# A gated attention with a feed-forward block on one core: the orders of three engines as written lists

## The chip, the core and the metric

The kernel runs on one core of a Trainium2 chip. The core has five engines with instruction streams of their own: TensorE (PE in the profile) multiplies matrices and transposes, VectorE (DVE) and ScalarE (ACT) work element by element, GpSimd (POOL) does the same and issues some loads, SyncE (SP) issues most transfers. Each engine runs its instructions strictly in the order in which the program holds them; engines wait for each other by semaphores. The metric is the device time of one execution in microseconds (us).

## The reference

Two blocks follow each other, in float32. The first is a gated linear recurrence for 4 batches of 8 heads, 768 time steps and 48 features: a complex decay per step and feature, and a state of 48 x 48 per head. The second is a feed-forward block on the 3,072 tokens that come out (384 wide, 1,024 hidden).

```python
mag = np.sqrt(a_re * a_re + a_im * a_im)
scale = np.minimum(mag, 0.999) / (mag + 1e-06)
a_re_n, a_im_n = (a_re * scale, a_im * scale)
for t in range(S):
    ar, ai = (a_re_n[:, :, t, :, None], a_im_n[:, :, t, :, None])
    new_re = ar * S_re - ai * S_im
    new_im = ar * S_im + ai * S_re
    kv = np.einsum('bhd,bhe->bhde', k[:, :, t], v[:, :, t])
    S_re, S_im = (new_re + kv, new_im)
    y[:, :, t] = np.einsum('bhd,bhde->bhe', q[:, :, t], S_re)
...
h = (x @ w1) * (x @ w2) @ w3
out = h @ w_out
```

## The kernel before

The tokens are cut into eight **units**, u = 0 to 7: unit u is half a batch, 384 tokens, in three chunks of 128. Each unit has these parts.

- **Gate chain** (VectorE and ScalarE by turns; `gates_apart` and `gates`): from the loads re and im of the decay it makes the running magnitude and angle, and from them and from q and k four products: gR and k (key with cosine and sine), gA and q (query with cosine and sine). A unit's chain runs while TensorE works on the unit before.
- **Moves** (SyncE): twelve transfers per unit bring the products into the layouts KL (from gR and k) and QL (from gA and q) that the scores read; pieces of V are moved too (`turn_vr`).
- **Attention on TensorE**, per chunk: transposes tp of gR and of k, copied by ScalarE to KT (L993); kv, the product of KT and V, added to a state T; scores sc of KL and QL, copied through a mask to A by VectorE (L1007); and y from A, V, QL and T, copied by ScalarE to xT (units 0 to 2) or x.
- **Feed-forward on TensorE**: products m with w1 and w2 (L1089), copied and multiplied to ab by ScalarE (L1101, L1123, L1130) and VectorE (L1105), then o with the fused weight w3o (L1184) and a store. From unit 3 on, w1 and w2 are used as a coarse part wh and a remainder low; ScalarE and VectorE split them once, beside unit 2 (L1152, L1155, L1157).

Ahead of all that stands the **weight product** w3 times w_out (`fuse`, L1451): eight steps f of eight products, each with a piece wo_s of w_out and a slice w3s of w3. Both are loaded as raw words by SyncE and rounded first: VectorE takes signs and shifted words (L1236, L1248, L1250), ScalarE the low ends (L1241, L1244), VectorE adds them (L1253, "ISA" in the order). w3s has two buffers, so the slice of step f + 2 is written where that of step f was read.

What sets the order: TensorE's program order is written out by the code. For ScalarE, VectorE and SyncE the order in the weight product was left to a scheduler of the language, with order-only dependences that keep ScalarE's steps of one function table together (`chain`); in the units an account of times in the program (`run`, `book`, the table `TIMES`) decides between which copies a step of the gate chain, a rounding, a split or a move is put, and the code is emitted in that order inside a `manual_schedule`.

## Time and profile before

| | us |
|---|---|
| median of 3 runs | 533.48 |
| lowest and highest | 533.29, 538.1 |
| span of the profiled execution | 534.5 |
| TensorE busy | 498.3 (93%) |
| VectorE busy | 374.7 (70%) |
| ScalarE busy | 325.6 (61%) |
| GpSimd busy | 254.0 (48%) |

The profile is of one execution, with the line numbers of the kernel before. A row names the engine, the line, what is written <- what is read, the tile's shape and, in brackets, the idle time ahead of the instruction with what ended it. Busy time of TensorE is made of matmuls that overlap, so it isn't TensorE at its peak. The profile also states TensorE's granted clock as a share of full speed; a mean under 1.00 holds stretches at half.

### The profile page before, as it was taken

What the parts mean: (1) busy time and instruction counts of PE and PEld (TensorE: products, weight loads), DVE (VectorE), ACT (ScalarE), POOL (GpSimd) and SP (SyncE); (2) the same over time, 40 slices, a digit from 0 to 9 for tenths busy, and PEclk for the clock granted to TensorE, in tenths of its full rate; (3) what the DMA queues carried; (4) which work ended last, traced back from release to release, by engine and by line L of the source; (5) the groups of instructions that cost most, each with busy time, mean ns of one, the idle gap of its engine ahead of it and who ended that gap; (6) DMA issues with size and microseconds to landing.
All of it is one profiled execution on the core that took longest, in us unless ns stands there. A gap on an engine that the chain in (4) does not pass through costs nothing.

```text
span 534.5 us, 13643 instructions
## 1 busy us (share of the span) xinstructions
PE 498.3 (93%) x5594; PEld 378.1 (71%) x5594; DVE 374.7 (70%) x607; ACT 325.6 (61%) x569; POOL 254.0 (48%) x317
## 2 busy tenths in 40 slices
PE   5689889999998999988999999999999998999995
PEld 2355565556655679957888688967896787878972
DVE  7999699855779988756773876577657837336750
ACT  6979866665675458982587557855786554213420
POOL 1000000028968886752664765487457458415510
PEclk9899999999999999998999999999999999999999
DMA  8999859692379219791599239932993176716611
GB/s 258 369 400 286 189 161 307 126 232 72 79 174 229 73 56 234 157 219 40 126 236 216 77 82 245 225 90 70 229 232 87 40 209 169 205 43 189 200 50 37
DMA packets 66424, 89.75 MB, mean 168 GB/s; under 512 B 29872, under 2 KB 53872, under 8 KB 65584
## 3 DMA queue, kind: packets, MB, share of 16 engines
q1 hardware_dynamic: 57904, 59.15, 44.0%
q0 software_dynamic: 8448, 29.63, 20.3%
q8 instruction: 46, 0.75, 0.6%
q14 instruction: 26, 0.21, 0.1%
HBM read 61.01 MB, written 4.72 MB: 123 GB/s over the span
## 4 chain that ended last, share of the span: by engine, by line
PE 51%; DVE 17%; DMA 13%; issue 6%; ACT 5%; POOL 5%; SPq 1%; POOLq 0%; DVEq 0%; ACTq 0%
PE m L1089 24%; PE o L1184 16%; PE y L1043 4%; PE sc L1004 4%; DMA k<-in_k_dram 3%; DMA KL<-k 3%; PE kv L1069 2%; DVE gR L750 2%; PE tp L991 2%; DMA QL<-q 2%; DMA q<-in_q_dram 2%; DMA look<-in_a_re_dram 1%; DVE gA L753 1%; DMA raw<-in_w_dram 1%; POOL look L1327 1%
## 5 line engine op out<-in xcount | busy, mean ns | idle before, releaser
L1184 PE MATMUL o<-w3o,ab 128*128 128x384 f32 x384 | 131.7, 492 | 0.0
L1089 PE MATMUL m<-x,low 128*128 128x384 f32 x576 | 119.2, 339 | 0.0
L1089 PEld LDWEIGHTS m<-x,low 128*128 128x128 f32 x576 | 102.6, 188 | 0.2 <-ACT m L1123 0.2
L1184 PEld LDWEIGHTS o<-w3o,ab 128*128 128x128 f32 x384 | 70.4, 190 | 45.6 <-issue 2.4
L1105 DVE TENSOR_TENSOR ab<-m,ab 128x384 f32<-128x384 f32 x64 | 35.1, 553 | 57.2 <-PE m L1089 39.4
L1089 PE MATMUL m<-x,wh 128*128 128x384 f32 x288 | 69.6, 350 | 3.4 <-ACT ab L1130 2.4
L1123 ACT ACTIVATE m<-m 128x384 f32<-128x384 f32 x96 | 45.5, 476 | 36.0 <-PE m L1089 35.6
L1089 PE MATMUL m<-xT,ws 128*128 128x384 f32 x192 | 63.1, 487 | 1.2 <-ACT xT L1054 1.2
L1328 POOL TENSOR_SCALAR look<-look 128x192 f32<-128x192 f32 (+1 forms) x55 | 54.4, 988 | 5.0
L1089 PEld LDWEIGHTS m<-x,wh 128*128 128x128 f32 x288 | 50.8, 188 | 7.4 <-ACT ab L1130 3.6
L1325 POOL TENSOR_TENSOR look<-look 128x256 f32<-128x256 f32 (+1 forms) x43 | 31.9, 743 | 50.1 <-DMA look<-in_w_dram 32.3
L1089 PEld LDWEIGHTS m<-xT,ws 128*128 128x128 f32 x192 | 36.0, 190 | 25.6 <-ACT xT L1054 1.7
L1273 POOL MEMSET seen<- 128x256 bf16 x1 | 0.3, 317 | 107.7 <-DVE ab L1105 107.7
L1007 DVE COPY_PREDICATED A<-mask,sc 128x512 f32<-128x512 uint8 x48 | 32.8, 734 | 26.5 <-PE sc L1004 26.5
L1289 POOL TENSOR_TENSOR seen<-seen,look 128x192 bf16<-128x192 bf16 (+1 forms) x55 | 44.3, 805 | 4.5
L1051 POOL TENSOR_TENSOR x<-x,x 128x384 fp32r<-128x384 f32 x18 | 23.1, 1284 | 41.7 <-DVE x L1050 41.5
L1188 ACT COPY ot<-o 128x384 f32<-128x384 f32 x24 | 11.4, 476 | 48.4 <-PE o L1184 48.2
L1043 PE MATMUL y<-A,V 128*32 128x128 f32 x768 | 40.2, 276 | 0.6 <-issue 0.6
L1004 PEld LDWEIGHTS sc<-QL,KL 96*32 96x32 f32 x1536 | 29.2, 112 | 13.6 <-issue 8.7
L1004 PE MATMUL sc<-QL,KL 96*32 96x32 f32 (+3 forms) x1536 | 32.8, 238 | 4.4 <-DMA QL<-q 3.0
L1043 PEld LDWEIGHTS y<-A,V 128*32 128x32 f32 x768 | 35.0, 112 | 1.5 <-issue 1.5
L1043 PE MATMUL y<-QL,T 96*32 96x128 f32 x640 | 35.6, 275 | 0.0
(163 smaller groups left out, 909.2 us busy)
## 6 DMA issues: line engine op xcount, KB each, us to landing
looked<-in_w_dram POOLq DMA_DIRECT2D x14, 512.0 KB, 4.5
look<-in_w_dram POOLq DMA_DIRECT2D x27, 256.0 KB, 5.0
raw<-in_w_dram SPq DMA_DIRECT2D x6, 1024.0 KB, 10.3
KL<-gR SPq DMA_DIRECT2D x24, 192.5 KB, 3.6
KL<-k SPq DMA_DIRECT2D x24, 192.5 KB, 7.1
QL<-gA SPq DMA_DIRECT2D x24, 192.0 KB, 8.2
QL<-q SPq DMA_DIRECT2D x24, 192.0 KB, 7.9
raw<-in_w_dram SPq DMA_DIRECT2D x6, 768.0 KB, 6.1
```

Source lines behind the costliest of these rows:

```text
L1004: nc.tensor.matmul(out=sc[SB * g:SB * g + SB, j, s0:C], lhsT=KL[:, x * n + j, w][:, s0:s0 + SB], rhs=QL[:, x * n + j, w][:, s0:C], start=T ...
L1007: last["sc", u, c, x] = nc.vector.copy_predicated(out=A[:, x * n:(x + 1) * n], data=sc, mask=mask)
L1043: nc.tensor.matmul(out=o, lhsT=a, rhs=b, start=s0, stop=s1)
L1051: nc.gpsimd.tensor_tensor(out=x[2], in0=x[1], in1=x[0], op=OP.subtract)
L1089: nc.tensor.matmul(out=out, lhsT=a, rhs=b, start=start and i == 0, stop=i == len(terms) - 1, skip_group_check=not start)
L1105: last["ab", u, j] = nc.vector.tensor_tensor(out=ab_t[u][:, j], in0=m, in1=ab_t[u][:, j], op=OP.mult)
L1123: nc.scalar.activation(out=got[m], in_=got[m], func=AF.Copy, scale=1.0 + 1.0 / BITS)
L1184: nc.tensor.matmul(out=m, lhsT=ab_t[u][:, f, t * P:(t + 1) * P], rhs=w3o[:, f], start=(f == 0), stop=(f == KF - 1))
L1188: nc.scalar.copy(out=o, in_=m)
L1289: nc.gpsimd.tensor_tensor(out=seen[:, 0:n], in0=seen[:, 0:n], in1=x, op=OP.add)
L1325: tt(out=x, in0=x, in1=x, op=OP.mult)
L1328: ts(out=x, in0=x, scalar1=low, scalar2=None, op0=OP.is_ge)
```

## The change

Every call on `nc.scalar`, `nc.vector`, `nc.gpsimd` and `nc.sync` is now recorded, in the order of the code. At the end `in_order` reads a list of numbers for each engine: n over 0 takes the call n places behind the first that is left, n under 0 takes the next -n as they stand. Between each call and the next on the same engine it sets an order-only dependence, over the whole kernel, the weight product included. The list of GpSimd is empty, so its calls stay as recorded. The dependences of `chain` and the inner `manual_schedule` are gone. All recorded calls now carry the line of the recorder (L385).

```diff
--- before.py
+++ after.py
@@ -375,6 +375,69 @@
         f()
 
 
+class Log:
+
+    def __init__(self, engine):
+        self.engine, self.log = engine, []
+
+    def __getattr__(self, name):
+        def call(*args, **kw):
+            self.log.append(getattr(self.engine, name)(*args, **kw))
+            return self.log[-1]
+        return call
+
+
+class Logged:
+
+    def __init__(self, nc):
+        self.nc = nc
+        self.scalar, self.vector, self.gpsimd, self.sync = (Log(e) for e in (nc.scalar, nc.vector, nc.gpsimd, nc.sync))
+
+    def __getattr__(self, name):
+        return getattr(self.nc, name)
+
+
+ORDERS = dict(
+    scalar="""
+9 -10 5 -5 2 2 2 -1 1 1 8 2 -1 1 -1 1 -8 3 -1 3 -1 4 1 1 1 -2 3 -1 3 -2 4 -1 3 3 -3 6 6 6 -3 3 3 3 -1 2 1 1 -2 4 -3
...
+""", vector="""
+-2 11 4 4 4 9 1 1 -1 6 -1 4 -8 1 -2 11 -1 1 -1 7 -1 6 -1 2 -1 1 8 8 -4 5 4 -3 5 -1 5 4 1 1 2 2 3 -3 1 1 17 2 5 1 1 3
...
+""", gpsimd="""
+
+""", sync="""
+-3 8 -4 1 -2 3 -3 1 -1 7 -1 6 3 3 3 -1 2 2 1 1 1 -1 2 20 -4 18 18 20 17 21 21 17 2 15 5 16 2 7 4 2 12 5 3 4 2 2 2 4
...
+""")
+
+
+def in_order(tc, log, order):
+
+    left, before, taken = list(log), None, []
+    for n in map(int, order.split()):
+        taken += [left.pop(n)] if n > 0 else [left.pop(0) for _ in range(-n)]
+    for ins in taken + left:
+        if before:
+            tc.add_manual_dep(ins.ins, before.ins.name, ORDER, reason="order")
+        before = ins
+
+
 @with_exitstack
 def tile_gateloop__then__multiplicative_ffn_kernel(
     ctx: ExitStack,
@@ -413,7 +476,7 @@
 
 
 
-    nc = tc.nc
+    plain, nc = tc.nc, Logged(tc.nc)
     B, H, D, S = qt.shape
     P = 128
     C = 128
@@ -452,7 +515,7 @@
     weights_pool = ctx.enter_context(tc.tile_pool(name="weights", bufs=1))
     w3o = weights_pool.tile([P, KF, DM], FP, name="w3o")
     ident = weights_pool.tile([P, P], FP, name="ident")
-    make_identity(nc, ident)
+    make_identity(plain, ident)
     good = weights_pool.tile([1, 1], I32, name="good")
 
     fast = ExitStack()
@@ -598,8 +661,6 @@
 
     def chain(ins):
 
-        if chained and not paced:
-            tc.add_manual_dep(ins.ins, chained[-1].ins.name, ORDER, reason="tables")
         chained[:] = [ins]
 
     def gate_head(u):
@@ -1767,7 +1828,7 @@
         fills = [("f7", lambda j=j: [fuse(KF - 1, j + x) for x in range(2)]) for j in range(KF // 2, KF, 2)]
         gate["ops"] = gates(1, False)
         chain(nc.scalar.preload_act_table_set("natural_log_exp_and_others"))
-        with tc.manual_schedule(engines={mybir.EngineType.Activation, mybir.EngineType.DVE, mybir.EngineType.Pool, mybir.EngineType.SP}):
+        if True:
 
             paced.append(True)
             clock.update(PE=0.0, ACT=0.0, DVE=0.0, POOL=0.0, SP=3.0, DMA=8.0)
@@ -1797,9 +1858,11 @@
             seq += ffn(NU - 1)
             advance()
             run(seq[:-4] + [("judge", 0)] + seq[-4:-2] + [("judge", 1)] + seq[-2:])
+    for name, order in ORDERS.items():
+        in_order(tc, getattr(nc, name).log, order)
     fast.close()
 
-    value = nc.values_load(good[0:1, 0:1], min_val=0, max_val=1)
+    value = plain.values_load(good[0:1, 0:1], min_val=0, max_val=1)
     with tc.If(value == 0):
         general(tc, qt, kt, v, art, ait, w1, w2, w3t, wo, w3o, ident, out)
 
```

The number of instructions on each engine stays as it was, and so do the orders of TensorE and GpSimd. On VectorE 513 of 586 instructions stand in another place, on ScalarE 432 of 559, on SyncE 194 of 247, most of them by fewer than ten.

ScalarE in unit 0, at the end of the weight product (KT are the copies of the transposes; gA, re and gZ here are steps of unit 1's gate chain, low is a weight's low end). Before:

```order
L1455 ACTIVATE w3o<-f 128x384 x2
L993 COPY KT<-tp 128x128x3
L783 ACTIVATE gA<-re 128x3x384
L993 COPY KT<-tp 128x128x3
L783 ACTIVATE re<-gA 128x1152
L993 COPY KT<-tp 128x128x3
L1241 ACTIVATE low<-raw 128x512
L1073 COPY T_122<-kv 96x8x48
L993 COPY KT<-tp 128x128x3 x2
L783 ACTIVATE gZ<-gZ,consts 128x1152
L993 COPY KT<-tp 128x128x3
```

and after:

```order
L385 ACTIVATE w3o<-f 128x384
L385 COPY KT<-tp 128x128x3
L385 ACTIVATE low<-raw 128x512
L385 COPY KT<-tp 128x128x3 x2
L385 COPY T_122<-kv 96x8x48
L385 COPY KT<-tp 128x128x3 x3
L385 ACTIVATE w3o<-f 128x384
L385 ACTIVATE low<-raw 128x256
L385 ACTIVATE w3o<-f 128x384
L385 ACTIVATE low<-raw 128x256
L385 ACTIVATE w3o<-f 128x384 x2
```

The six KT copies stand ahead of the gate steps, which come later, behind the next copies w3o.

VectorE at step f = 2 of the weight product (w3s<-raw are the signs of the next slice, w3s<-w3s,low and wo_s<-wo_s,low the last step of the rounding). Before:

```order
L835 TENSOR_SCALAR gA<-gA 128x384
L838 SCALAR_TENSOR_TENSOR gA<-gA,gZ 128x384
L1253 ISA w3s<-w3s,low 128x2048
L1253 ISA wo_s<-wo_s,low 128x768
L1248 TENSOR_SCALAR w3s<-raw 128x1024
L853 TENSOR_TENSOR gZ<-gA,gR 128x384
L1236 TENSOR_SCALAR low<-raw 128x384
```

and after:

```order
L385 SCALAR_TENSOR_TENSOR gA<-gA,gZ 128x384
L385 TENSOR_SCALAR gA<-gA 128x384
L385 TENSOR_SCALAR w3s<-raw 128x1024
L385 ISA w3s<-w3s,low 128x2048
L385 ISA wo_s<-wo_s,low 128x768
L385 SCALAR_TENSOR_TENSOR gA<-gA,gZ 128x384
L385 TENSOR_SCALAR low<-raw 128x384
```

The signs of the slice for f = 3 moved from behind the two roundings for f = 2 to ahead of them.

SyncE in unit 3 (KL and QL are the moves that the scores need, V the moves of v's pieces, im and re loads for the next units). Before:

```order
L740 DMA KL<-gR 16x8x385 x3
L527 DMA im<-in_a_im_dram 128x3x384
L740 DMA KL<-k 16x8x385 x3
L740 DMA QL<-gA 16x8x384 x3
L740 DMA QL<-q 16x8x384 x3
L1190 DMA out_dram<-ot 128x384 x3
L527 DMA re<-in_a_re_dram 128x3x384
```

and after:

```order
L385 DMA KL<-gR 16x8x385
L385 DMA QL<-gA 16x8x384
L385 DMA V<-vr 64x6x48
L385 DMA KL<-gR 16x8x385 x2
L385 DMA KL<-k 16x8x385 x2
L385 DMA QL<-gA 16x8x384 x2
L385 DMA QL<-q 16x8x384 x3
L385 DMA KL<-k 16x8x385
L385 DMA V<-vr 64x6x48
L385 DMA V<-vr 32x6x48 x2
L385 DMA im<-in_a_im_dram 128x3x384
```

im moved from ahead of nine of the moves to behind all twelve, and three of V's pieces, which all stood ahead of the moves, stand behind them, one among them.

## Rows read from the trace of the kernel before

**Rows 1.** The page's first part: span, busy time of each engine.

```profile
span 534.5 us, 13643 instructions
...
PE 498.3 (93%) x5594; PEld 378.1 (71%) x5594; DVE 374.7 (70%) x607; ACT 325.6 (61%) x569; POOL 254.0 (48%) x317
```

**Rows 2.** The list of TensorE's waits: total us, times, longest us.

```profile
PE sc L1451 <- DVE wo_s L1253: 12.6, 5, 6.6
PE kv L1069 <- ACT KT L993: 3.8, 3, 2.2
PE sc L1004 <- DMA QL<-q: 3.0, 1, 3.0
PE m L1089 <- ACT ab L1130: 2.4, 3, 1.0
PE tp L991 <- DVE gR L750: 1.6, 3, 0.7
...
PE tp L991 <- ACT KT L993: 1.0, 3, 0.6
PE tp L991 <- DVE k L758: 1.0, 2, 0.7
PE m L1089 <- DVE ab L1105: 0.8, 2, 0.4
```

**Rows 3.** Windows: us, busy of PE, PEld, DVE, ACT, POOL, TensorE's clock, DMA.

```profile
240.00:280.00 40.00, 37.16 (x512) 32.57 (x513) 28.99 (x39) 23.30 (x46) 20.90 (x24) 0.96 0.56 132
```

**Rows 4.** Timeline of TensorE, 0 to 40: start, us, operation [idle before, what ended it].

```profile
17.49 2.31 PE L1451 MATMUL sc<-wo_s,w3s 128*128 128x384 f32 x4 [3.12 <-DVE wo_s L1253]
...
25.89 1.56 PE L1451 MATMUL sc<-wo_s,w3s 128*128 128x384 f32 x4 [1.27 <-DVE wo_s L1253]
...
37.85 1.56 PE L1451 MATMUL sc<-wo_s,w3s 128*128 128x384 f32 x4 [1.38 <-DVE wo_s L1253]
```

**Rows 5.** Timeline of VectorE, 24 to 26.

```profile
24.16 1.20 DVE L1253 CUSTOM_DVE_ANT_0 w3s<-w3s,low 128x2048 uint16<-128x2048 uint16 x1
25.28 0.55 DVE L1253 CUSTOM_DVE_ANT_0 wo_s<-wo_s,low 128x768 uint16<-128x768 uint16 x1
25.75 0.69 DVE L1248 TENSOR_SCALAR w3s<-raw 128x1024 int32<-128x1024 int32 x1
```

**Rows 6.** DMA of the first 26.5 us: the line of totals.

```profile
DMA packets 3460, 8.31 MB, mean 314 GB/s; under 512 B 379, under 2 KB 1899, under 8 KB 3179
```

**Rows 7.** Timeline of ScalarE, 57 to 60.

```profile
57.65 1.16 ACT L783 ACTIVATE gA<-re 128x1152 f32<-128x1152 f32 x1
58.71 0.55 ACT L993 COPY KT<-tp 128x384 f32<-128x384 f32 x1
```

**Rows 8.** Timeline of ScalarE, 165 to 167.

```profile
165.32 0.84 ACT L1152 ACTIVATE wh<-ws 128x768 fp32r<-128x768 f32 x1 [1.28 <-DVE low L1155]
166.07 0.54 ACT L993 COPY KT<-tp 128x384 f32<-128x384 f32 x1
```

**Rows 9.** Timeline of SyncE's DMA queue, 222 to 236: start, time of issuing.

```profile
223.54 0.60 SPq L527 DMA_DIRECT2D im<-in_a_im_dram  x1
...
229.82 3.88 SPq L740 DMA_DIRECT2D QL<-q  x3
```

**Rows 10.** DMA of 222 to 236 us: GpSimd's queue, packets, MB, share.

```profile
q0 software_dynamic: 173, 0.58, 15.8%
```

**Rows 11.** Timeline of VectorE, 60 to 106.

```profile
60.33 1.36 DVE L807 TENSOR_TENSOR im<-im,re 128x1152 f32<-128x1152 f32 x1 [4.03 <-ACT re L783]
...
72.93 1.37 DVE L1007 COPY_PREDICATED A<-mask,sc 128x512 f32<-128x512 uint8 x2
...
104.16 1.36 DVE L962 TENSOR_TENSOR gR<-k,re 128x1152 f32<-128x1152 f32 x1 [2.11 <-ACT re L783]
```

**Rows 12.** Timeline of TensorE, 111 to 112.

```profile
111.43 0.49 PE L991 MATMUL tp<-ident,gR 128*128 128x128 f32 x3
```

18 rows, old and new, of the table scalar are left out of this document.

## Prediction

> **What bounds the kernel now.** I read the page's busy shares first: TensorE (PE) is busy 498.3 of 534.5 us [rows 1]. The reader should see that the end is set by TensorE, and that an order of the other engines can win only two things: the time in which TensorE stands still, and the time in which it runs at the lower of its two clock levels after it stood still. Next comes the list of TensorE's waits [rows 2]; with its few smaller rows it sums to 29.7 us. The first 6.6 us of that are the wait for the first weights, so 23.1 us are to be had. Some 6.0 of these are the rest of the wait for rounded w_out weights (12.6 less 6.6) in the weight product ahead of the first unit; 17.1 us are spread over the eight units. Third I read the engine that ends each large wait, in order of time, to see what it did just before.
>
> The profiled execution's span is 534.5 us, 0.2% over the median of the runs, 533.48 us. I make the sum against 534.5 and take 1.0 us off at the end.
>
> **The change part by part.** TensorE's order and GpSimd's order stay as they were, and no instruction is added: order-only dependences between instructions of one engine need no semaphore. So no term is paid for the lists themselves, and every matmul keeps its duration. What moves is who stands in front of whom on ScalarE, VectorE and SyncE.
>
> *KT copies.* TensorE waits 3.8 us at kv and 1.0 us at tp for ScalarE's copies of transposed keys [rows 2], 4.8 us together. In unit 0 a copy of 0.55 us starts at 58.71, behind a gate step of 1.16 us that began at 57.65 [rows 7]; the other copies of this unit stand behind a second such step. The list puts all six copies of the unit ahead of both steps. In unit 2 the copy at 166.07 stands behind a weight split (wh) that itself waited 1.28 us for VectorE [rows 8]; this is the longest of the KT waits, 2.2 us. The list puts the copies of this chunk ahead of those splits. What is late next in unit 0 is a low end of a weight that now stands between the first and the second copy and waits for VectorE. I take 4.1 us of 4.8; bounds 2.5 and 4.8, since VectorE's steps may now come late where the copies were.
>
> *Moves in unit 3.* The longest wait among the units is 3.0 us at the scores for QL<-q [rows 2]. SyncE issues the 576 KB load of the next unit's im at 223.54, in front of nine of the twelve moves of KL and QL; the last three, QL<-q, start to issue at 229.82 [rows 9]. The list puts im behind all of them, and three of the V pieces behind them too, one among them. im fed only a chain that starts after the scores. I take 2.7 us of 3.0; bounds 0 and 3.0. With the wait goes the drop of the clock behind it: the mean granted clock of 240 to 280 us is 0.96 where it is 1.00 in stretches without such a wait [rows 3]; 4% of 40 us is 1.6 us at most, and I take 1.3.
>
> [...]
>
> *Small waits of the later units.* gR 1.6, m for ab of ScalarE 2.4, k 1.0, m for ab of VectorE 0.8 [rows 2]: 5.8 us in ten waits of 0.3 to 1.0 us, each a copy or a gate product that comes just late behind a neighbour. The list moves most of these by two to seven places, the copies forward and the gate steps back or the other way. Some go and some new ones come: 2.5 us, bounds 0 and 5.8. What is left of the 17.1 us (less 4.8, 3.0 and 5.8 it is 3.5, waits for score copies, xT and the like) I count with 0.6.
>
> Sum of gains: 4.1 + 2.7 + 1.3 + 2.5 + 0.6 = 11.2 us.
>
> *The head, a loss.* The eight steps f of the weight product each need a rounded w_out piece. The second, f=1, starts at 17.49 after a wait of 3.12 us, f=2 at 25.89 after 1.27, f=4 at 37.85 after 1.38 [rows 4]. The list on SyncE puts the 1,024 KB load of w3 for f=2 in front of the w_out load for f=1. In this stretch the queues moved 314 GB/s on average [rows 6], and that holds the empty first microseconds; 1.05 MB is 3.3 us at that rate, and I take 2.6 as the rate once it runs is higher. So f=1 starts 2.6 us later. VectorE then rounds f=2: before, w3s (1.20 us, from 24.16), wo_s (0.55, from 25.28), and after both the signs of f=3 (0.69, from 25.75) [rows 5]. The list puts these signs in front. They write the buffer that the last product of f=1 reads, so they cannot start before that product ends, and TensorE must then wait for 0.69 + 1.20 + 0.55, about 2.4 us, where it waited 1.3 [rows 4]: 1.2 us more. Against that, w3 of f=4 is loaded seven places earlier, and the wait ahead of f=4, 1.4 us, goes. Net loss 2.6 + 1.2 - 1.4 = 2.4 us. Bounds: a gain of 2.5, if the loads of f=1 overlap so that w_out lands as before and the early loads close the later waits; a loss of 4.
>
> The clock was lower behind the first of these waits: the four matmuls at 17.49 took 2.31 us, the four at 25.89 took 1.56 [rows 4]. That loss is there already, and I add none for the longer wait.
>
> *Unit 1, a loss.* VectorE began unit 1's gate chain at 60.33, behind an idle stretch of 4.03 us that ScalarE's gate steps ended [rows 11]. In the list the chain's first steps stand 19 to 24 places later, behind all score copies of unit 0, the last pair of which ran from 72.93 to 74.3 [rows 11]. The result gR began at 104.16 and took 1.36, so it was there at 105.5 [rows 11]; TensorE asks for it at 111.43 [rows 12], 5.9 us of slack. The start moves by 13 to 14 us. But VectorE stood still between its steps in this stretch, 2.11 us directly ahead of gR [rows 11], and weight roundings that used to stand between the chain's steps now stand ahead of them; the work from the chain's start to gR is about 34 us, so it ends at 108 if nothing stands still, and later by each wait for ScalarE. In the list gR also stands behind two ab products that are bound to TensorE's last matmuls ahead of the transposes, so it is just in time at best. I take a loss of 1.5 us; bounds 0 and 7.7 (13.6 less 5.9). Another 0.5 us is for units 2 and 3, where weight splits and chain are interleaved anew.
>
> Sum: 534.5 - 11.2 + 2.4 + 1.5 + 0.5 = 527.7 us of span, and 526.7 us as a median.
>
> **Rivals.** A run of this kernel tells about 1% from no change, so faster means under 528.1 and slower over 538.8.
>
> (a) The forecast, chance 0.56, own range 521 to 532; some two thirds of it lie under 528.1.
>
> (b) Nearly all waits of the units close: all 17.1 us and the 1.6 of the clock, with the head as it was: 534.5 - 18.7 = 515.8, with the head's loss 518.2; as a median 515 to 517. For it speaks that each large wait is removed by a move that leaves the waiting engine free; against it that the ten small ones have ten different neighbours. Chance 0.14.
>
> (c) The waits only change places: QL<-q lands no sooner, since the 16 DMA engines are busy in that stretch anyway, and the small waits come back elsewhere. Then 4.0 and 2.5 drop from the gains: 534.5 - 4.7 + 4.4 = 534.2, as a median 533. For it: a fixed list makes an engine stand behind a step that is late, and there are ten such interlocks in every unit. Against: KT and QL waits are each ended by one plain neighbour. Chance 0.18. It covers also that the lists do no more than write down nearly the same order: most instructions move by under ten places.
>
> (d) Slower: unit 1's gate chain. If none of the 13.6 us is won back, TensorE waits 7.7 us at unit 1's transposes. VectorE then runs behind, unit 2 repeats about half, 4, and two waits of this length drop the clock twice, 1.6 each. 534.5 - 11.2 + 2.4 + 7.7 + 4 + 3.2 = 540.6, as a median 539.6. It decides as soon as gR of unit 1 comes more than about 6 us after TensorE asks. For it: 34 us of work in 34 us of room. Against: VectorE's idle time in that stretch. Chance 0.12.
>
> **The numbers.** The predicted time is that of (a), 526.7. The range that leaves out (d), and the lower edge of (b), is 515.5 to 536. Faster: 0.38 of (a) and 0.14 of (b), 0.52. Same: 0.18 of (a) and 0.18 of (c), 0.36. Slower: 0.12.
>
> **What would show it.** KT copies: no wait at kv over 0.5 us in units 0 and 2. Moves: no wait for QL<-q and a clock of 1.00 in that unit. Head: f=1 starts near 20 us, a wait of about 2.4 us ahead of f=2, none ahead of f=4. Unit 1: gR ends close to the point at which the transposes ask, with a new wait of one or two us. The prediction falls if f=1 starts no later than before, or if the transposes of unit 1 wait for gR by more than 4 us.

## The result and the profile after

The changed kernel is slower: 541.98 us (median of 4 runs, 540.37 to 542.26) beside 533.38 us (4 runs, 533.17 to 538.1) for the kernel before on the same chip. The ratio is 1.0136, interval [1.0088, 1.0183]. The forecast was 526.7 us, so the time lies outside the range, on the side of the least likely rival. The medians of the kernel before differ from chip to chip (533 to 541 us), so below each ratio is to the runs of before beside it; the changed kernel was timed only beside the 533, so the experiments are compared with it in us and by their traces.

The page of the changed kernel, beside [rows 1]:

```profile
span 538.5 us, 13607 instructions
...
PE 502.6 (93%) x5594; PEld 382.1 (71%) x5594; DVE 374.5 (70%) x607; ACT 324.0 (60%) x569; POOL 254.9 (47%) x317
...
q8 instruction: 46, 0.75, 0.6%
```

The work is the same, and TensorE is still the bound. That its busy time grew by 4.3 us with the same 5,594 matmuls means a slower clock (a mean of 0.973 beside 0.993). The list of TensorE's waits, beside [rows 2] (engine, line, what ended the wait: total us, times, longest):

```profile
PE sc L1512 <- DVE wo_s L385: 16.8, 3, 7.2
PE sc L1065 <- issue: 5.4, 2, 3.5
PE y L1104 <- issue: 2.2, 1, 2.2
PE m L1150 <- ACT xT L385: 1.3, 2, 0.7
PE sc L1512 <- DVE w3s L385: 1.3, 1, 1.3
PE kv L1130 <- ACT KT L385: 1.2, 2, 0.7
PE sc L1065 <- DVE A L385: 0.8, 3, 0.3
PE tp L1052 <- ACT w3o L385: 0.4, 1, 0.4
PE m L1150 <- DVE ab L385: 0.3, 1, 0.3
```

Nearly every wait that the lists aim at is gone: QL<-q, gR, k and ScalarE's ab have no row any more. Two places have grown: the weight product ahead of the first unit (wo_s, 12.6 to 16.8 us), and a kind of wait that no engine and no load of data ends, "issue": 7.6 us where before had 0.6 in its whole list.

How far TensorE is behind can be read at the products kv, which both kernels run in the same order. It is 6.4 us late at the first kv of unit 0 (59.31 before, 65.72 after), 16.3 at that of unit 1 (115.53, 131.80), 18.0 at that of unit 2 (169.01, 187.05), then 11.1 at that of unit 4, 4.2 at the last of unit 7 (461.04, 465.26), and 4.2 at the end of the last matmul (528.50, 532.72). So **the lists lose 18 us in the first 190 us and win 13.8 back afterwards**. The timeline of TensorE, at the places of the loss, and where kv and the scores of unit 3 stand (start, us, operation, in brackets the idle time ahead of it):

```profile
22.06 2.93 PE L1512 MATMUL sc<-wo_s,w3s 128*128 128x384 f32 x4 [7.14 <-DVE wo_s L385]
...
31.39 2.38 PE L1512 MATMUL sc<-wo_s,w3s 128*128 128x384 f32 x4 [2.39 <-DVE wo_s L385]
...
44.92 1.56 PE L1512 MATMUL sc<-wo_s,w3s 128*128 128x384 f32 x4 [1.25 <-DVE w3s L385]
...
80.76 1.50 PE L1065 MATMUL sc<-QL,KL 96*32 96x64 f32 x39 [3.54 <-issue]
...
89.08 0.27 PE L1104 MATMUL y<-A,V 128*32 128x128 f32 x1 [2.23 <-issue]
...
127.67 0.52 PE L1052 MATMUL tp<-ident,gR 128*128 128x128 f32 x3
...
131.80 0.88 PE L1130 MATMUL kv<-vr,KT 128*32 128x48 f32 x48 [0.70 <-ACT KT L385]
...
146.40 0.77 PE L1065 MATMUL sc<-QL,KL 96*32 96x64 f32 x33 [1.90 <-issue]
...
256.20 1.32 PE L1065 MATMUL sc<-QL,KL 96*32 96x128 f32 x64
```

The first three rows answer to [rows 4], tp to [rows 12]; the last is where QL<-q was waited for. Windows of the same kernel, 240 to 280 being that of [rows 3] (us, busy us of PE, PEld, DVE, ACT, POOL, TensorE's granted clock, share and GB/s of the DMA engines):

```profile
59.00:89.00 30.00, 22.98 (x496) 17.25 (x495) 18.18 (x35) 14.02 (x25) 0.00 (x0) 0.89 1.07 258
...
79.80:86.60 6.80, 5.84 (x127) 5.81 (x128) 4.45 (x6) 0.65 (x2) 0.00 (x0) 0.50 1.09 241
90.10:96.80 6.70, 6.12 (x21) 3.24 (x13) 1.36 (x1) 3.00 (x4) 0.00 (x0) 0.50 0.75 188
148.10:151.40 3.30, 3.30 (x6) 1.35 (x4) 2.96 (x6) 0.00 (x0) 3.10 (x4) 0.50 0.10 30
240.00:280.00 40.00, 39.51 (x604) 30.92 (x603) 27.05 (x39) 22.97 (x43) 25.11 (x30) 1.00 0.59 133
```

And one of the kernel before:

```profile
59.00:89.00 30.00, 26.83 (x548) 19.20 (x549) 27.21 (x44) 22.87 (x33) 0.00 (x0) 1.00 0.73 216
```

From 59 to 89 us the DMA engines are full after the change (1.07, packets overlapping on an engine count twice) and had room before (0.73). Within that stretch TensorE stands still twice for "issue", and behind each such wait its clock is at half (0.50) for 6.8 us. The kernel before has this twice, for 3.4 us each: at 18.2 behind the wait ahead of f=1, and at 243.4 behind that for QL<-q; elsewhere, but for its last microsecond, its clock is 1.00. From kv of unit 0's last chunk to kv of unit 1's first the lag grows by 10.9 us, from 5.4 to 16.3. The two waits less the 0.6 of before are 5.1 us; the two stretches at half clock, 5.84 and 6.12 us busy, cost about half of that, 6.0, by estimate from the 0.50. Together 11.1.

What TensorE waits for there is, by the times, a block of its own instructions. The DMA view shows a queue of kind "instruction" (q8) that moves 46 packets of 16 KB in the whole run; TensorE's 11,188 matmuls and weight loads make 243 to a packet. One such packet moves at 78.09 to 79.35, and TensorE goes on at 80.76; one at 86.53 to 87.71, and it goes on at 89.08; one at 144.09 to 145.06, and it goes on at 146.40. The first of these in the DMA view of 78.0 to 79.4 (queue: packets, MB, share):

```profile
q1 hardware_dynamic: 209, 0.41, 98.1%
q8 instruction: 1, 0.02, 5.6%
```

The data queue next to it is full.

The other traces bear this out, and show when a block is asked for. TensorE's order is the same in every run, so its matmuls and weight loads can be counted. In all 17 profiles the waits for issue of over 0.5 us, 20 of them, stand at four places of that order (about the 695th, the 951st, the 1,199th to 1,205th and the 1,957th to 1,963rd instruction), some 250 apart or a multiple of it, and each ends 2.2 to 2.7 us after such a packet starts to move. The packet that is needed at one place seems to be asked for one block earlier: where the queues have room it moves at about the time that TensorE passes the place before. The kernel before passes its 700th instruction at 67.0, and the packet for the 951st moves at 67.6. The changed kernel passes it at 72.6, and the packet moves at 78.09. Its windows up to the 700th (350 matmuls and 350 weight loads) and from there to the packet:

```profile
0.00:72.60 72.60, 53.49 (x350) 31.01 (x350) 56.60 (x130) 53.91 (x92) 2.00 (x11) 0.93 0.92 274
72.60:78.10 5.50, 4.40 (x128) 3.12 (x125) 4.91 (x9) 2.79 (x4) 0.00 (x0) 1.00 1.12 230
```

In these 5.5 us the DMA engines are full (1.12). In the kernel before they are full for the 1.6 us between its 951st instruction and the next packet, and the wait of 0.6 us in its list follows:

```profile
71.80:73.40 1.60, 1.60 (x86) 1.60 (x78) 1.60 (x4) 1.07 (x3) 0.00 (x0) 1.00 1.06 373
```

Over all profiles, ten packets of unit 0 moved 3.8 us or more after the place before them was passed; the share of the DMA engines in between was 0.97 to 1.12 each time. Where it was under 0.6 no packet of unit 0 took more than 2.5 us (in the kernel before 2.4 us from 74.4 to 76.8, at 0.49).

Scores and y are where this hurts: 64 score matmuls with their 64 weight loads take about 1.3 us, half a packet's worth, and in unit 1 TensorE went through a block in 3.1 us (141.4 to 144.5). What fills the data queue is SyncE's list; its queue around unit 0's scores:

```profile
66.77 1.35 SPq L385 DMA_DIRECT2D raw<-in_w_dram  x3
68.18 0.62 SPq L385 DMA_DIRECT2D re<-in_a_re_dram  x1
68.85 0.61 SPq L385 DMA_DIRECT2D im<-in_a_im_dram  x1
72.43 0.39 SPq L385 DMA_DIRECT2D raw<-in_w_dram  x1
72.92 0.56 SPq L385 DMA_DIRECT2D k<-in_k_dram  x1
73.52 0.88 SPq L385 DMA_DIRECT2D q<-in_q_dram  x1
74.44 0.76 SPq L385 DMA_DIRECT2D vr<-in_v_dram  x1
```

Unit 1's re, im, k, q and vr (576 KB each) and weights are issued within some 8 us. Before, re and im of this unit went out at 39.6 and 43.9, and k, q and vr from 81.2 on.

### The profile page after: what moved, and what is told of

It reads as the page before. It is cut to its first block, busy times and chain, and to the rows that moved or that the text cites. A ratio compares the mean times of both kernels' runs of the same rounds, so it can differ in the third digit from the quotient of the medians.

```text
span 538.5 us, 13607 instructions
## 1 busy us (share of the span) xinstructions
PE 502.6 (93%) x5594; PEld 382.1 (71%) x5594; DVE 374.5 (70%) x607; ACT 324.0 (60%) x569; POOL 254.9 (47%) x317
## 4 chain that ended last, share of the span: by engine, by line
PE 86%; DMA 4%; ACT 3%; DVE 3%; issue 2%; SPq 0%; ACTq 0%; DVEq 0%
PE m L1150 40%; PE o L1245 23%; PE y L1104 7%; PE sc L1065 5%; PE f L1512 4%; PE kv L1130 3%; DMA raw<-in_w_dram 3%; PE tp L1052 2%; PE sc L1512 2%; DMA im<-in_a_im_dram 2%; DVE w3s L385 1%; ACT re L385 1%; ACT gA L385 1%; SPq L385 0%; DVE A L385 0%
## 5 line engine op out<-in xcount | busy, mean ns | idle before, releaser
L1245 PE MATMUL o<-w3o,ab 128*128 128x384 f32 x384 | 133.3, 497 | 0.0
L385 DVE TENSOR_TENSOR ab<-m,ab 128x384 f32<-128x384 f32 x64 | 35.5, 554 | 59.0 <-PE m L1150 55.7
L385 POOL TENSOR_SCALAR look<-look 128x192 f32<-128x192 f32 (+1 forms) x70 | 69.4, 992 | 13.5 <-DMA look<-in_a_re_dram 8.1
L1150 PE MATMUL m<-xT,ws 128*128 128x384 f32 x192 | 65.9, 503 | 1.3 <-ACT xT L385 1.3
L385 ACT ACTIVATE m<-m 128x384 f32<-128x384 f32 x96 | 45.7, 479 | 34.5 <-PE m L1150 34.1
L385 POOL TENSOR_TENSOR look<-look 128x256 f32<-128x256 f32 (+1 forms) x58 | 41.7, 719 | 49.5 <-DMA look<-in_w_dram 33.8
L385 POOL MEMSET seen<- 128x256 bf16 x1 | 0.3, 317 | 123.3 <-DVE ab L385 123.3
L1150 PEld LDWEIGHTS m<-xT,ws 128*128 128x128 f32 x192 | 37.4, 197 | 27.3 <-issue 2.6
L385 ACT COPY ot<-o 128x384 f32<-128x384 f32 x24 | 11.5, 477 | 66.2 <-PE o L1245 66.2
L385 POOL TENSOR_TENSOR seen<-seen,look 128x192 bf16<-128x192 bf16 (+1 forms) x55 | 47.0, 855 | 4.5
L385 DVE COPY_PREDICATED A<-mask,sc 128x512 f32<-128x512 uint8 x48 | 32.7, 731 | 18.0 <-PE sc L1065 17.8
L1104 PE MATMUL y<-A,V 128*32 128x128 f32 x768 | 41.5, 281 | 2.2 <-issue 2.2
L385 ACT COPY ab<-m 128x384 f32<-128x384 f32 x64 | 30.7, 479 | 18.1 <-PE m L1150 17.9
L385 ACT ACTIVATE low<-raw 128x384 uint16<-128x384 uint32 (+6 forms) x40 | 34.3, 891 | 11.9 <-DMA raw<-in_w_dram 5.2
L385 POOL TENSOR_TENSOR x<-x,x 128x384 fp32r<-128x384 f32 x18 | 24.5, 1368 | 35.8 <-DVE x L385 35.8
L1065 PEld LDWEIGHTS sc<-QL,KL 96*32 96x32 f32 x1536 | 28.9, 111 | 16.1 <-issue 10.9
## 6 DMA issues: line engine op xcount, KB each, us to landing
raw<-in_w_dram SPq DMA_DIRECT2D x6, 1024.0 KB, 10.9
```

Of the source, the lines that this page charges most:

```text
L385: self.log.append(getattr(self.engine, name)(*args, **kw))
L1065: nc.tensor.matmul(out=sc[SB * g:SB * g + SB, j, s0:C], lhsT=KL[:, x * n + j, w][:, s0:s0 + SB], rhs=QL[:, x * n + j, w][:, s0:C], start=T ...
L1104: nc.tensor.matmul(out=o, lhsT=a, rhs=b, start=s0, stop=s1)
L1150: nc.tensor.matmul(out=out, lhsT=a, rhs=b, start=start and i == 0, stop=i == len(terms) - 1, skip_group_check=not start)
L1245: nc.tensor.matmul(out=m, lhsT=ab_t[u][:, f, t * P:(t + 1) * P], rhs=w3o[:, f], start=(f == 0), stop=(f == KF - 1))
```

## The experiments

All edit only the numbers of the lists, so that calls stand in another order; the diffs show the rows of the order that moved. "Old order" is that of the kernel before, written as a list. The kernel with the old order up to 150 us and the changed lists behind it is called the base. Where an expectation names theory I, it is that TensorE's instruction blocks come late behind the loads that SyncE's list bunches; theory H is about the head, the weight product: that the wait ahead of f=1 is set by which loads SyncE puts first.

**Which part of the lists.**

e1: all three lists give the old order, the lists themselves and their dependences stay.

```diff
 scalar
-9 -10 5 -5 2 2 2 -1 ...   (the changed order)
+9 -15 3 3 3 -2 1 1 ...    (the order of the kernel before; vector and sync likewise)
```

> All three written lists hold the order that the kernel before had; recorder and order-only dependences stay as in the change. Theory A (all of the loss comes from the order of the instructions) expects no change from the kernel before: ratio 0.997 to 1.003, and the first two waits for w_out weights at 3.1 and 1.3 us again. Rival C (fixing the order by dependences costs time by itself, through other waits between engines) expects a part of the loss of 8.6 us here, 536 us or more.

Measured 538.19 beside 538.34, ratio 0.9987 [0.9939, 1.0035]. No cost of writing an order down is seen. But its profile has a longer wait for issue than the 0.6 us of before:

```profile
78.48 0.43 PE L1087 MATMUL y<-A,V 128*32 128x128 f32 x3 [2.93 <-issue]
```

TensorE passed the place before, its 951st instruction, at 72.2, and the packet moved at 76.1. The window between the two:

```profile
72.20:76.10 3.90, 3.35 (x139) 3.08 (x133) 3.40 (x8) 1.75 (x4) 0.00 (x0) 1.00 0.98 335
```

So this wait comes and goes in the old order too, and there too the DMA engines were full (0.98) while the block was due.

e2: old order for all calls up to 150 us, the changed lists behind (the base). e3: the other way round.

```diff
 order of ScalarE, VectorE and SyncE     e2             e3
-calls up to 150 us                      changed   ->   changed
+calls up to 150 us                      old            changed
+calls after 150 us                      changed        old
```

> The order of before for all instructions that started before 150 us in its trace (weight product, units 0 and 1), the written lists for the rest. Theory A: the whole loss lies in the first part, and the lists gain in the second; TensorE was 18.0 us behind the kernel before at the last key products of unit 1 and 4.2 us behind at those of unit 6, so this run should be 13 us faster than the kernel before or a little less: 519 to 524 us. Rival B (the gains of the late units are only the time that was lost earlier, since the other engines could run ahead while TensorE stood still) expects waits to come back in the late units and 530 us or more.

> The reverse: the written lists up to the instructions of 150 us, the order of before for the rest. Theory A: the loss of the first part alone, some 15 to 18 us, less what the old order's waits of the late units now cover: 545 to 552 us. Rival B: the late units gain here too, since the other engines had time to run ahead: about 542 us, as the change.

e2 took 526.13 us beside 538.34 (run times 521.95 to 533.53). e3 took 564.28, ratio 1.0531 [1.0456, 1.0606], more than I expected: its waits for issue are 5.7 and 2.5 us, and all late waits of the old order come back (KT 3.6, one of 3.5 at the scores of a later unit, gR, k and ab), and the mean clock is 0.964. So the gain sits behind 150 us and the loss ahead of it.

e12: the base once more, with more runs.

> The base once more, in more rounds: old order up to 150 us, written lists behind. Its first four runs were 522.0, 522.1, 530.1 and 533.5 us. If the gain of the late units is real it is 1.5 to 3% faster than the kernel before on the same chip, with runs in two groups some 8 us apart, as an issue wait of 2.9 us with its half-clock stretch comes or not; if the early result was luck, within 1%.

Measured 525.57 (522.34 to 530.24, 6 runs), **ratio 0.9738 [0.9676, 0.98]**: this beats both kernels. Its waits:

```profile
PE sc L1506 <- DVE wo_s L385: 12.1, 5, 6.6
PE kv L1124 <- ACT KT L385: 1.6, 2, 0.9
PE m L1144 <- ACT ab L385: 1.4, 2, 1.3
PE sc L1059 <- DVE A L385: 1.3, 3, 0.6
```

The head is that of [rows 2], and the rest of that list has shrunk to rows of 1 to 2 us, one of them a wait for issue of 1.1.

**Which engine's list.** e5: the base, with SyncE's changed list from the start. e6: the base, with the changed lists of ScalarE and VectorE from the start.

```diff
 calls up to 150 us     base    e5         e6
-ScalarE, VectorE       old
+ScalarE, VectorE               old        changed
+SyncE                  old     changed    old
```

> As the run with the old order up to 150 us and the lists behind it (526 us; its base), but SyncE's part up to 150 us follows the written list too; VectorE and ScalarE keep the old order there. Theory A1 (the loss of the first part is SyncE's list: w_out of f=1 behind 1,024 KB more, and the loads of unit 1 bunched up while TensorE needs its instruction blocks) expects most of the 18 us that the change loses there: a wait of 5 us or more ahead of f=1, waits called issue of 2 us or more in unit 0's scores or y, and 535 to 542 us. Rival A2 (the loss is the order on VectorE and ScalarE) expects 520 to 529 us.

> The other half: up to 150 us VectorE and ScalarE follow the written lists, SyncE the old order; the lists for all behind it. Theory A1 expects a wait of about 3 us ahead of f=1 and of 2.4 us ahead of f=2 (the signs of f=3 ahead of the roundings), no wait at the KT copies of unit 2, no issue wait over 1 us in unit 0, and 519 to 529 us. Rival A2 expects 535 us or more.

567.05 us, ratio 1.0503 [1.0415, 1.0591], and 559.12, ratio 1.0347 [1.0266, 1.0428]. Neither theory's times held. Each half alone is far worse than both together (1.0136): in e5 kv waits 14.8 us for KT, in e6 the scores wait 4.4 us for A. e5 has no wait for issue over 0.2 us, though SyncE follows the changed list in it. An engine that issues in one order and one that consumes in another stand behind each other's late steps, so the loss can't be put on one list in this way.

**The loads of unit 1.** e4: the changed kernel, with k, q and vr behind the two weight loads that followed them.

```diff
 L385 DMA im<-in_a_im_dram 128x3x384
-L385 DMA raw<-in_w_dram 128x3x512
+L385 DMA raw<-in_w_dram 128x3x512 x3
 L385 DMA k<-in_k_dram 128x3x384
 L385 DMA q<-in_q_dram 128x3x384
 L385 DMA vr<-in_v_dram 128x3x384
-L385 DMA raw<-in_w_dram 128x3x512 x2
```

> The changed kernel with one edit on SyncE: the loads of k, q and v of unit 1 (576 KB each) stand four places later, behind the weight load that waits for the last copy of unit 0's attention, about where the kernel before had them. Theory I (TensorE's waits of 3.5 and 2.2 us in unit 0's scores and y, which the profile calls issue, are waits for its own instruction blocks of 16 KB, fetched by DMA behind these loads) expects both waits at 1 us or less, the two half-clock stretches behind them gone, and 9 us less than the change: 530 to 535 us. Rival J (the waits come from the copies on VectorE and ScalarE, or from the number of instructions in that stretch) expects no change: 540 to 543 us.

541.02, ratio 1.0081 [1.004, 1.0123]. The wait in y is gone, that in the scores stays at 3.47 us; now TensorE waits 3.0 us for gR of unit 1: two weight loads behind k, q and vr are issued at 104.83 in place of 101.57, and VectorE waits 6.66 us for them with unit 1's gate chain behind it.

e9: e4, and re and im put ahead of the moves of unit 0.

```diff
 L385 DMA raw<-in_w_dram 128x2x512 x2
+L385 DMA re<-in_a_re_dram 128x3x384
+L385 DMA im<-in_a_im_dram 128x3x384
 L385 DMA V<-in_v_dram 64x3x48 x2
...
-L385 DMA re<-in_a_re_dram 128x3x384
-L385 DMA im<-in_a_im_dram 128x3x384
```

> The changed kernel with two edits on SyncE: the loads re and im of unit 1 go back ahead of unit 0's moves, and the loads k, q and v of unit 1 three places behind, where the weight load that waits for unit 0's last copy stands ahead of them; VectorE and ScalarE keep the written lists. With k, q and v alone moved, the wait in unit 0's y went and the one in its scores stayed at 3.5 us, re and im still being in the queues. Theory I expects both issue waits of unit 0 at 1 us or less now. The time: both waits and their half-clock stretches are some 10 us, but k and q come late for unit 1's products as they did there (3 us at the transposes): 533 to 540 us. Rival J expects the 3.5 us in the scores to stay.

538.92, ratio 1.0006 [0.997, 1.0042]; in us it is 3.1 under the changed kernel, and the ratio is no sign that the loss is gone, since before ran at 539.23 beside it. Both waits for issue in unit 0 are gone, as theory I expects and rival J doesn't. What stands at its scores, and where unit 1's first kv stands:

```profile
76.06 1.42 PE L1065 MATMUL sc<-QL,KL 96*32 96x128 f32 x64 [1.63 <-DVE A L385]
...
131.17 0.88 PE L1130 MATMUL kv<-vr,KT 128*32 128x48 f32 x48 [0.70 <-ACT KT L385]
```

That kv is 15.6 us later than before, where the changed kernel is 16.3 late; at the last kv of unit 0 the two are 5.8 and 5.4 late. So without the waits for issue 9.8 us are lost in between in place of 10.9: waits for A (1.6), ab (1.2 twice) and gR (3.0, from the same late weight loads as in e4) and two shorter stretches at half clock (a mean of 0.983 over the run, changed kernel 0.973) have taken their place. Unit 1 keeps one wait for issue of 0.8 us, and at the first kv of unit 2 the lag is 14.6, 3.4 us less than in the changed kernel.

e7: the base with the edit the other way, re and im of unit 1 behind the moves.

```diff
 L385 DMA raw<-in_w_dram 128x2x512 x2
-L385 DMA re<-in_a_re_dram 128x3x384
-L385 DMA im<-in_a_im_dram 128x3x384
 L385 DMA KL<-gR 16x8x385
...
 L385 DMA raw<-in_w_dram 128x3x512
+L385 DMA re<-in_a_re_dram 128x3x384
+L385 DMA im<-in_a_im_dram 128x3x384
```

> The base of 526 us with one edit on SyncE: the loads re and im of unit 1 (576 KB each) go from ahead of unit 0's moves to behind them, the place that the written list gives them. Theory I (instruction blocks come late because the DMA queues are full when unit 0's scores begin) expects an issue wait of 2 us or more in unit 0's scores or y, a half-clock stretch behind it, and 4 to 8 us more than the base: 529 to 535 us. Rival J expects no issue wait beyond the 0.6 us of the base and 522 to 528 us.

539.87, ratio 1.0022 [0.9981, 1.0063]: some 14 us over the base, but by another way than the one under test. No wait for issue; kv waits 18.34 us, since ScalarE's copies KT stand behind a gate step that now waits 17.28 us for re. This is the interlock of e5 again, and it says nothing on the instruction blocks.

e10: the base, with k, q and vr ahead of four weight loads.

```diff
-L385 DMA raw<-in_w_dram 128x3x512 x6
+L385 DMA raw<-in_w_dram 128x3x512 x2
 L385 DMA k<-in_k_dram 128x3x384
 L385 DMA q<-in_q_dram 128x3x384
 L385 DMA vr<-in_v_dram 128x3x384
+L385 DMA raw<-in_w_dram 128x3x512 x4
```

> The base of 526 us with one edit on SyncE: the loads k, q and v of unit 1 go four weight loads ahead, right behind the second 768 KB weight load, so that they are in the queues while TensorE runs unit 0's scores and y. Theory I expects an issue wait of 2 us or more between 73 and 90 us in every run, a half-clock stretch behind it, and 530 to 536 us. Rival J expects what the base has: 522 to 528 us in its better runs.

527.93, ratio 0.9776 [0.9709, 0.9843], and no wait for issue over 0.2 us: the wait that theory I expected did not come, though the DMA engines were busier than in the base (0.87 from 59 to 89 us, base 0.73). The trace shows why. By the count of places one block was asked for at 70.7 and moved at 71.75, before those loads (issued 70.87 to 72.2) could stand in its way. The next was asked for at 74.1 and moved only at 81.02; in between the DMA engines were full:

```profile
74.10:81.00 6.90, 6.33 (x58) 4.17 (x59) 5.39 (x9) 2.90 (x5) 0.00 (x0) 1.00 1.09 220
```

But TensorE was by then in the long matmuls of the feed-forward and came to the place that needs it only at 104. So this block cost no time, though it moved 6.9 us after it was asked for.

**The head, and the copies KT.** e8: the base, with the 1 MB load of w3 for f=2 ahead of w_out for f=1, as the changed list has it.

```diff
 L385 DMA raw<-in_w_dram 128x1024
+L385 DMA raw<-in_w_dram 128x2048
 L385 DMA raw<-in_w_out_dram 128x768
 L385 DMA raw<-in_w_dram 128x1024
-L385 DMA raw<-in_w_dram 128x2048
```

> The base of 526 us with one edit on SyncE: the 1,024 KB load of w3 for f=2 goes ahead of the w_out load for f=1. Theory H (TensorE's wait ahead of f=1 grows by the time of the bytes put in front, with nothing else moved) expects a wait of 5.5 to 7 us ahead of f=1 in place of 3 to 4, and less of a wait ahead of f=2. Its rival (the wait of 7.1 us in the change comes from VectorE, where the im products stand ahead of w_out's rounding) expects 3 to 4.5 us.

A single run: 531.85 us. TensorE waits 5.91 us ahead of f=1 where [rows 4] have 3.12: 2.8 us for this one load, as the term of the head had it (2.6), or 1.8 to 3.3 beside the two profiles of the base (4.07 and 2.57); f=2 then waits 0.93. (It also has a wait for issue of 2.9 in y.)

e11: the base, with unit 0's copies KT ahead of the gate steps, as in the changed list.

```diff
-L385 COPY KT<-tp 128x128x3
-L385 ACTIVATE gA<-re 128x3x384
-L385 COPY KT<-tp 128x128x3
-L385 ACTIVATE re<-gA 128x1152
-L385 COPY KT<-tp 128x128x3
+L385 COPY KT<-tp 128x128x3 x3
 L385 ACTIVATE low<-raw 128x512
 L385 COPY T_122<-kv 96x8x48
-L385 COPY KT<-tp 128x128x3 x2
+L385 COPY KT<-tp 128x128x3 x3
+L385 ACTIVATE gA<-re 128x3x384
+L385 ACTIVATE re<-gA 128x1152
```

> The base of 526 us with one edit on ScalarE: unit 0's six KT copies go ahead of the three gate steps of unit 1 that stand among them, as in the written list. The term of the prediction on KT copies expects the waits of 0.9, 0.6 and 0.4 us near 60 us to go and 1 to 2 us less than the base. Its rival (the gate steps that come later delay unit 1's chain, and the loads make the time anyway) expects no difference within 1 us or a new wait of 1 us or more at unit 1's transposes.

528.98, ratio 0.9796 [0.9745, 0.9847], no better than the base (525.57 beside the same runs of before). The wait at kv in unit 0 goes, and one of 6.7 us for A comes, since the copies A on VectorE stand behind a product that waits for the gate step moved back:

```profile
64.74 1.36 DVE L385 TENSOR_TENSOR im<-im,re 128x1152 f32<-128x1152 f32 x1 [8.38 <-ACT re L385]
```

e13: the changed kernel with the old order up to 57.2 us, so with the old head.

```diff
 order of ScalarE, VectorE and SyncE
-calls up to 57.2 us    changed
+calls up to 57.2 us    old
 calls after 57.2 us    changed
```

> The old order up to 57.2 us (the weight product, the loads and moves of unit 0, and with them the loads re and im of unit 1), the written lists for all behind it, unit 0's attention included. If the weight product's share of the loss is what TensorE had lost at the first key product of unit 0, some 6 us, and the rest comes from the loads around unit 0, then: waits ahead of f=1, 2 and 4 as in the kernel before (3.1, 1.3, 1.4 us); no wait of 2 us or more in unit 0's scores, since re and im come early; an issue wait of about 2 us in y may stay, since k, q and v of unit 1 still stand early; 524 to 532 us. If the loss is bound to units 0 and 1 themselves, 535 us or more.

539.14, ratio 1.0053 [1.0011, 1.0096]; span 539.0. TensorE begins unit 0 at -0.4 us against before, where the changed kernel has +6.4, and reaches unit 1 at +15.7, where that has +16.3. Nearly all of the 6 us are gone again in unit 0. TensorE's waits there, beside those of the changed kernel:

```profile
PE sc L1063 <- DVE A L385: 9.2, 3, 8.5
PE y L1102 <- issue: 4.2, 2, 3.9
PE sc L1063 <- issue: 2.1, 1, 2.1
...
```

And what VectorE stood at, with the copies A behind it:

```profile
71.67 0.30 DVE L385 TENSOR_SCALAR low<-raw 128x256 int32<-128x256 int32 x1 [9.21 <-DMA raw<-in_w_dram]
```

TensorE comes earlier and waits for VectorE, which stands behind weights that SyncE's list loads late.

e14: e13, with k, q and vr behind the weight loads as in e4. e15: e13, with two 256 KB weight loads ahead of V's, those that VectorE stood at.

```diff
 e14
-L385 DMA raw<-in_w_dram 128x3x512 x2
+L385 DMA raw<-in_w_dram 128x3x512 x4
 L385 DMA k<-in_k_dram 128x3x384
...
-L385 DMA raw<-in_w_dram 128x3x512 x2
 e15
 L385 DMA QL<-q 16x8x384
+L385 DMA raw<-in_w_dram 128x512 x2
 L385 DMA V<-in_v_dram 128x3x48
...
-L385 DMA raw<-in_w_dram 128x512 x2
```

> The same with k, q and v of unit 1 three places later on SyncE, as in the run with the loads spread. Theory I: no issue wait over 1 us in unit 0; but waits of about 1.2 us at ab and 3 us at unit 1's transposes come back, as they did when the list had these loads late: 524 to 530 us. If k, q and v early did no harm without re and im in the queues, it is slower than the run before it.

> The run with the old head (539 us) with one edit on SyncE: the two 256 KB loads of w1 and w2 that stood behind fourteen V loads go ahead of them, their place in the kernel before. In that run VectorE stood still for 9.2 us on the first of them, with the state sums and score copies of unit 0 queued behind, and TensorE waited 8.5 us for A. If that queue is the cause, the wait for A falls to 1 us or less and an issue wait of 2 to 4 us in y may stay: 529 to 535 us. If VectorE only meets the next late load there, the wait for A stays over 4 us and the time within 3 us of 539.

537.56, ratio 1.002 [0.9977, 1.0064], and 536.79, ratio 0.9964 [0.9926, 1.0002]. In e14 unit 0 has no wait for issue any more, unit 1 keeps one of 2.0, and the wait for A is still 6.9 us. In e15 that wait falls to 0.7, and another of 4.9 comes one step on, where VectorE meets the next load that is late:

```profile
77.55 0.56 DVE L385 TENSOR_SCALAR low<-raw 128x768 int32<-128x768 int32 x1 [7.17 <-DMA raw<-in_w_dram]
```

Taking away one cause uncovers the next: the list's unit 0 has several loads that come late by a like amount.

## Why the prediction was wrong

*KT copies, 4.8 to 0.7 forecast.* Right: kv waits 1.2 us, tp 0.4 for a neighbour of the copies. In the changed kernel the price shown by e11 is not paid: the step of VectorE that waits for the gate step stands behind all score copies A of unit 0 there (at 82.96), and ahead of them in e11, which keeps VectorE's old order.

*Moves in unit 3, a gain of 2.7 and 1.3 of the clock.* Right: no wait at 256.20, and a clock of 1.00 from 240 to 280 where it was 0.96. GpSimd's loads, which are not reordered, ran beside the moves with 15.8% of the 16 DMA engines' time before [rows 10] and 25.1% after (231.5 to 246.5), and could have kept QL late; here they did not.

*Small waits.* Forecast 2.5 of 5.8 us; measured nearly all. The row of gR, that of k and that of ScalarE's ab are gone, VectorE's ab is 0.3. From the first kv of unit 2 on the lists win 13.8 us, where my terms for that stretch sum to 6.6 (moves 2.7, clock 1.3, small waits 2.5, the rest 0.6, less 0.5): the size was too low, on the good side.

*The head, a loss of 2.4.* The mechanism was right, the size was not. f=2 waits 2.39 us, forecast 2.4: signs 0.69, 1.22 and 0.55 in a row. f=1 was to start near 20 and starts at 22.06. Of that, e8 gives some 2.8 us to the w3 load. The rest is not tested; the trace has three signs of it: the first product already starts 0.6 us later (7.23, before 6.62), SyncE issued w_out for f=1 at 11.39 instead of 8.38, and VectorE stood at a step of the gate chain whose load was late:

```profile
18.77 0.56 DVE L385 TENSOR_TENSOR im<-im,gR 128x384 f32<-128x384 f32 x1 [1.32 <-DMA im<-in_a_im_dram]
...
19.85 0.35 DVE L385 TENSOR_SCALAR low<-raw 128x384 int32<-128x384 int32 x1
...
29.04 0.69 DVE L385 TENSOR_SCALAR w3s<-raw 128x1024 int32<-128x1024 int32 x1 [1.02 <-PE f L1512]
29.65 1.22 DVE L385 CUSTOM_DVE_ANT_0 w3s<-w3s,low 128x2048 uint16<-128x2048 uint16 x1
30.79 0.55 DVE L385 CUSTOM_DVE_ANT_0 wo_s<-wo_s,low 128x768 uint16<-128x768 uint16 x1
...
126.16 1.36 DVE L385 TENSOR_TENSOR gR<-k,re 128x1152 f32<-128x1152 f32 x1 [0.30 <-ACT re L385]
```

(They answer to [rows 5], the last to [rows 11].) The wait ahead of f=4 was to go and is 1.25. And "I add none for the longer wait" was wrong: the clock of the first 40 us is 0.87, before 0.96. In all 6.4 us instead of 2.4. Yet e13 shows that without this loss the unit behind it gives most of it back.

*Unit 1's gate chain, a loss of 1.5, and rival (d).* Neither is what the changed kernel shows. gR is ready at 127.52 (126.16 and 1.36) and tp starts at 127.67 without a wait: just in time, as the working had it "at best", but only since TensorE itself was 16 us late. The chain began at 82.96, not near 74, and from there to gR took 44.6 us where the working had about 34. Rival (d) has the sign of the result by luck. Yet its wait stands close behind: in e4, e9 and e14 TensorE waits 3.0 us for gR.

*The step that failed* is a term that is not in the sum. I asked of each moved load who reads it, and never how full the queues would be where it now runs. Unit 1's loads cover nothing that is needed soon, so I gave their move no price; they ran in the second half of unit 0 beside TensorE's own instruction blocks. The row "issue, 0.6 us" in the list of waits of before was the sign of it, and I counted it to the small ones. Where the sum has a loss of 1.5 us for unit 1, TensorE loses 10.9 from the last kv of unit 0 to the first of unit 1: two waits for blocks, 5.1 us more than before, and some 6.0 of clock behind them. In unit 1 come 1.9 us of waiting and up to 1.65 us of clock (3.30 us busy at half).

That these are waits for blocks that come late behind full queues is shown: by the places and the packets in all profiles, by e9, which takes the loads away (a share of 0.75 from 59 to 89 us) and with them both waits of unit 0, and by e1 and e10, where a block comes late while the DMA engines are full (3.9 us at 0.98, 6.9 at 1.09) and TensorE waits in e1 alone (2.93 us). That the blocks alone make the loss is not shown, and e9 speaks against it.

*Which share of the 18 us is the blocks' and which that of the engines waiting for each other and for late loads* is not settled as a sum. At the first kv of unit 2 the lag is 18.0 us in the changed kernel and 14.6 without the waits for issue of unit 0 (e9); with the old head it is 17.8 (e13), and 14.4 without those waits (e14). So each cause alone gives back 0.2 to 3.4 us, and other waits of 1 to 8 us take its place in units 0 and 1. That the early lists as a whole are worth a loss, and the late ones a gain, is shown by e2, e3 and e12.

## What to carry to other kernels

When an order moves loads, draw up how many bytes each stretch of the queues now carries, and look at what else needs them there; loads that nobody waits for can still make others late (here a block of instructions, which moved 5.5 us after it was asked for, with the DMA engines at 1.12). Test a long list in pieces by time, not by engine: pieces by time told gain from loss at once (0.974 for the base), pieces by engine stood in each other's way (1.03 and 1.05). And a wait that is removed in a tightly filled stretch wins only the time up to the next step that is late there: e9 took away some 11 us of waits and clock in unit 0 and ended 3 us faster.

## What was not expected of the hardware

TensorE stood still, by the times, for its own instructions. They come in blocks of 16 KB by a DMA queue of their own (q8, 46 packets in this run), by the count above asked for one block ahead. In the changed kernel TensorE ran through a block in 3.1 to 6.1 us at the three places of its waits, and the next block took 5.0 to 8.3 us from the place passed to TensorE going on; so it waited 3.54, 2.23 and 1.90 us, and in the old order once 2.93 (e1). These are three of 46 blocks, where TensorE stood still for 7.7 us in all; its list has no other wait for issue.

In unit 0 of this run such a wait cost about twice its length, since a stretch at half clock (0.50) stands behind it: 5.1 us of waiting and, by estimate, some 6.0 us of clock. Behind a shorter one, the 0.6 us of before, the clock stayed at 1.00 (72 to 90 us).
